# First batch in quarters of columns, one-pass k sketches and shared logits in a sketched-attention and expert-attention kernel

## The chip, the cores and the metric

The kernel runs on one core of a Trainium2 chip. The metric is the device time of one execution in microseconds (us). Engines are named as in the profile: PE is TensorE's matmul, PEld its weight load, DVE is VectorE, ACT is ScalarE, POOL is GpSimd, SP is SyncE, which here issues nearly all DMAs.

## What is computed

The first half is attention by polynomial sketches (4 batches, 4 heads, 1088 positions, width 32, sketch size r = 8, all float32):

```python
def phi(x):
    a = np.einsum('rd,bhsd->bhsr', S1, x)
    b = np.einsum('rd,bhsd->bhsr', S2, x)
    return np.einsum('bhsi,bhsj->bhsij', a, b).reshape(*x.shape[:-1], r * r)
q_p, k_p = (phi(q), phi(k))
kv = np.einsum('bhsf,bhsd->bhfd', k_p, v)
z = np.sum(k_p, axis=2)
num = np.einsum('bhsf,bhfd->bhsd', q_p, kv)
den = np.einsum('bhsf,bhf->bhs', q_p, z)[..., None] + 1e-06
```

Its result, heads side by side, is x (4, 1088, 128). The second half is causal softmax attention with 4 experts, of which each position uses the 2 with the largest logits:

```python
logits = x @ w_gate
topk = np.argpartition(-logits, K, axis=-1)[..., :K]      # K = 2
...
for e in range(E):                                          # E = 4
    scores = scale * ((x @ wq[e]) @ (x @ wk[e]).transpose(0, 2, 1))   # causal mask, softmax -> a
    ye = a @ (x @ wv[e]) @ wo[e]
    out += share_of_expert_e_at_each_position * ye
```

## The kernel before, in words

**Order.** The kernel defines about 1275 small jobs (`job(...)`, each with its engine or a choice of two, what it reads, what it makes and which buffers it holds) and then runs them in the order of a list written out at the top, `ORDER` (lines 21 to 69). A number is a job; "a" or "b" behind it picks the engine. Each engine runs its own jobs strictly in that order, and so does SP with its DMA issues. Buffers come from small pools: 4 PSUM pairs (`ps`), 6 of `w`, 3 of `fp`, and so on. So the list decides both the queues and which buffer is free when.

**Four batches**, each prepared (`prepare`) and then attended (`batch`: `queries`, `scores`, `values`, `outputs`), the preparation of one lying between the attention of the one before.

**Preparation.**
- `sketch` (L501 to L516): q and k, transposed in 32 x 32 blocks by DVE, are multiplied by the sketch matrices in 32 x 32 tiles of the array (L515). The sketch matrix is held as a high and a low part, so each sketch is two passes. Batch 0 does this in two cuts of columns: 34 columns of 32 are split as 4 x 8 columns plus a remainder of 2, so there are 32-wide and 256-wide matmuls; later batches have 288-wide ones.
- `turn_sketch` (L519, DVE) turns the sketches back, `features` (L524, POOL or DVE) makes the 64 products, `sums` (L555, PE) makes kv and z.
- Batch 0 (`attend_rows`): `turn_features` (L589), `numer` (L612: 18 full-array matmuls of 128 rows, the sums of two heads in a block-diagonal tile `kvz`), `divide` (L619 to L621), `turn_x` (L627), `keep_x` (L630 to L635), stores to DRAM (`xd`).
- Later batches (`attend_turned`): the k sums are repeated to all row groups by 4 matmuls with a 0/1 matrix `rep4` (`repeat_sums`, L690) and copied (`keep_repeated`); a fifth sketch column (`fifth`, L696) gives the denominator; `weigh`, `invert`, `scale_first` divide the sketch, then features, `turn_f` (L733), `numer` (L755).
- `choose_experts`: `logits` (L805: 4 matmuls per part of columns, each part computed for both halves of the partitions), `turn_logits` (L809), then comparisons, masks (`store_masks` L890, `fetch_masks` L895: through DRAM, spread to all partitions) and shares (`shares`, `scale_shares`).

**Attention**, three groups of 6, 6 and 5 tiles of 64 positions: `queries` (L958, `pick` L971), `scores` (L996), `take` (L1008, DVE), `soften` (L1024, ACT), `weigh` (L1039, POOL), `turn` (L1044, DVE), `values` (L1072), `outputs` (L1143, L1169, L1193).

**Start of the program.** DVE decodes the sketch matrices; PE runs dummy matmuls (L247: 6 of the 40 dummy jobs are placed, 5 of them before the first sketch); SP and ACT issue the loads of q and k in two parts, SP those of v.

Of the kernel before, what the change touches and what calls it, by code (L numbers as in the profile page):

```python
# [21 lines left out]
0 3 46 4 1 2 48 76 77 82 51 75 42a 22a 49 87 50 45 26b 88 59 86 21a 74 5a 60 16a 61 78 79 54 96 85 81 62a 97 98 89 99a  # L22
80 102a 100b 101a 91 395 107 394 392 83a 84b 111 109 58 391 108a 53 90 24b 66 95a 94b 403 113 112a 110a 92a 393 56 52
104 93b 63 404 103 115 65 106a 105a 117 114b 55 47 398 396 116a 399 402 64 400 401 67b 405 684 121 118 125 407 68 70 406
122 411a 119 126 397 410a 69 57 687 10b 409b 25b 123 127 408a 413 412 124b 13b 120b 414b 130 128a 150 146 31b 151 148
147 416 131 686 154 420a 180 415 149 152 419a 153 155 179 417 162 184a 132 167 168 170 156 418a 163 158 159b 157a 133
181 183a 182 129 169 185 186 421 187 164 165 423 692 215 166a 194 188 422 189 246 195 689 190a 196 216 217 138 191 174
430 424 171 192 431 197a 245 208 432 425 426 428a 209 427a 249a 201 172 685 173 218a 193 202 198 222 247 219 248 223 160
318 250a 251 136 252 429 161a 220 433a 319 224 323a 37b 225a 221 276 434a 175 275 226 322a 277 71 141 140 134 435 176
253 73 8a 203 199 72 321 9b 204a 278 320 254 279b 436 694 227 210 255 324 695 325 438a 256b 177 143 228 205 292 211a  # L30
437a 291 698 456 178a 212 257 293 206 200 258 207 268 700 699 690 137 458 294 213 703a 214 267 457 269 139 701a 260 261
135 280 459 259 284 688 283 229 230 231 460 281 295b 702b 704a 36b 691 270 271b 233a 693 461 262 467 285 272 273 237 706
263b 705 296 462 234a 235a 282 463 297 142 696 232a 286 351 350 697 707b 236 709 708 710 298 711a 713a 327 264 343 352
287b 326 239 265 40b 353 274 342 982 238 712a 714 354a 288 266 328 986 289 473 344 345 468 715 355 290 717 329 472 356
144 475 474 477a 716 19b 723 439 299 464 330b 476a 985 979 443 300 301 346a 302 347 980 331 469 478 303 304 724 357 307a
479 348 334 332 442 335 333 358 977 470 471a 440 306a 718 359 308a 305b 310 309 336 719 311 361 360 725 337 362 508 978
338a 363 441 145 509 364a 312 541 540 510 339 501 983 349 487 315 502 503 504a 365 340 341 313 480 314 366 488 44b 367
316a 481 539 465 511b 538 721a 489 368 726a 543a 720b 722 17b 369 988 512 370 371 513 372 542b 505 373 445 506 490b 374
727a 514 981 544 375 376 545 568 491 377a 569 380a 728 378a 379a 507 482 447 381 444 383 570 553 492 317 571 554 576 382
494 495 483b 577 496 34b 484 987 493 497a 498 578 729 485 555 731a 486 515 384 516 730b 579 584 585 499 586 517 500 518a  # L40
991 519 749 993 750 612 520 751 521 32b 546 587 556a 611 547 992 580a 615a 241 754 385 572a 752 581 557 989 996a 446 558
559 613 614 466 548 573 549b 386 242 240 448 616a 574 760 617 588b 450 589 550 753 453 984 582 997a 583 761 33b 522 451
551 618 29b 523 524 243b 525a 561 528a 628 575 590 995b 452 560 454 526a 529 762 530 627 652 532 755 527a 629 562 651
654 591 653 994a 563 552 564a 531 619 388 655 630 656 620 643 621 631b 635 565 644 622 766 566 763 244 636 645 567 637
657a 632 646 658 756 767 455 623b 765 768 633 592 593 647b 449 659 594 595 770b 624 596 597 757 764a 638 732 769b 648
736 771 772 634 649 639a 601a 533 625 660 598a 650 599a 787 640 602 734 535 641 788 780 794 534 789 603 600b 735 795 604
626 808 536a 733 781 801 642 389 782 773 998 802 605 809 810 999 661 11b 783a 662 663 387 737 1000b 664 665 774 775 803
666 811a 990 1002 43b 804b 667 758 668 796 669 790b 812 784 6b 671a 813 785 739 797a 805 1001 1003 1005a 1006b 831 673a
1004a 832 672b 670a 791 834 814 836a 798 675 833 792 744 799 674 835a 12b 806 786 1007 738 837 838 1009 677 1008 676 905
1016 846 847 800 793 839 776b 28b 853 854 840 741 848 777 807 855 904 841 1010 849a 907 909a 537 778 878 850 851 740 856  # L50
1017 908a 877 1018 779 1011 842b 879 759 861 843 880 862 1012 743 1019b 881a 863 857a 844 906 678 910 1014a 815 864 858
816 845 911 865a 817 27b 1013a 1020a 390 818a 819a 679 869 1015 921 870 1021 882 883 859 35b 823 680 820a 821b 920 7b
822 852 866 681 871 922 1022 606 867 1024a 1023a 936 868 937 884 945 872 860 1042 944 938 1043 912 1044 15b 824 873b 30b
1047 747 929 913 1045 746 874 928 608 742 825 607 923 1046 914 748 930 947 1132 875 1048 939 946 1129 915 948 1131 609a
876 916b 1130 940a 1025 1053 1049 1134b 917 949 950a 885 1051 931 1133b 745 886 918 1027 951 887 941 1026 942 888 932a
610 952 924a 1028 919 889 890 933 39b 1135 934 828 953 827 925 1029 1054 892b 1136 896 826 943 891a 1176 894a 829a 1175
893b 14b 897 926 935 1137 1177 1151 1152 1055 1159 895 1144 1178 1153 1160 898 1204 1138 927 1145 1202 1161 1203 1179b
1139 1207b 1206a 1205 1162 1154 1180 954 955 956 1146 1155b 1056 957 958 1052 1057b 1208 1156 1181 18b 959 960 1147a 961
1163a 1182 1035 1164 1148 1140b 962 1209 1227 1165 963a 1167 1141 1166 967 1030 830 1142 965b 683 966a 1226 1168 1149
964a 968 1228 1169 1157 1143 1235 1033 1234 970 1236 1031 1219 1037 1218 969 1229 1220 1058 1170 1237 1171a 1150 1050  # L60
1230b 899 1242 1158 1243 1172 1231 1244 1040 1059 38b 23b 1039 682 1061 1221 901 1210 1232 1211 900 1222a 1233 1062b
1063b 1064 1238b 1212 902a 1060 1245 1065 1173 1174 971 1032 1223 1213 1246 1224 1073 1214a 972 1080 1215 1247 1041 1081
1074 1239 1225 1216 1240 1082 1248a 1087 1249 1217 1094 1095 1083a 1036 1034 1250 1241 1088 1183 1075 1251 1184 1084
1089 1185 1101 1066 1186 1067 1068 1102 973 1187 976 1252 1076b 1188 1038 1069a 1253 1103 974 1189a 1104b 1070 1193 1105
1085 1096 1077 1190b 41b 903 1254 1071 1255 1194 1090a 1097a 1256 1191b 1106 1091 1196 1192a 1257 1098 1195 1258 1259
1260 1198 1099 1264a 1107 1078 1072 1261b 1100 1086 1197 1265 1092 1262a 1263a 1079 1199 1267 1093 1108 1109 1110 1266
# [48 lines left out]
def kernel(  # L115
# [80 lines left out]
    def a_us(n):  # L196
        return 0.2 + 0.00073 * n
# [209 lines left out]

    pieces_of = {}  # L410

    def prepare(b, rank):
        early = b == 0
# [869 lines left out]
```

## Time and profile before

| what | us |
|---|---|
| median of 3 runs | 270.88 (270.36 to 271.32) |
| the profiled execution | 270.75 |
| its span, first to last instruction | 269.0 |
| PE busy, its weight loads busy | 259.9, 196.3 |
| DVE, POOL, ACT busy | 215.3, 154.2, 101.8 |

The span is what the profile shows; the execution's own time is 1.75 us more. Busy times are of one engine each and overlap. A matmul that waits in PE's pipeline can count as busy, so the weight loads (PEld) are shown beside it. A row of the chain of waits gives the start, the length, the engine, the tile written (pair is a PSUM pair), the line and the count of instructions; each float32 matmul of L515, L555, L612 and most others is two instructions, each with a weight load of its own.

### The profile page before, as it was taken

Reading aid. Unit: us, or ns where it says so; the run is one execution under the profiler, and the core shown is the slowest. Engines: PE = TensorE matmul, PEld = TensorE weight load, DVE = VectorE, ACT = ScalarE, POOL = GpSimd, SP = SyncE. Lnnn points to the kernel's source line nnn. Section 1 sums busy time; section 2 is a strip of 40 time slices with the busy share of each in tenths; the row PEclk is TensorE's granted clock in tenths of the full one; section 3 lists DMA queues with packets and bytes.
Section 4 is the critical chain, followed back from the end, with each engine's and each line's share of the span. In section 5 each row is a group of like instructions: output and inputs, shape, how many; then the busy total and the mean of one; then the engine's idle time right before and its main releaser. Section 6 shows DMA issues by size and latency. Waiting matters only on the chain.

```text
span 269.0 us, 9743 instructions
## 1 busy us (share of the span) xinstructions
PE 259.9 (97%) x4081; PEld 196.3 (73%) x4081; DVE 215.3 (80%) x536; ACT 101.8 (38%) x275; POOL 154.2 (57%) x245
## 2 busy tenths in 40 slices
PE   8599989999999999999999999999999999999994
PEld 3388846557586896586499976764796885789994
DVE  5887799999979986989998249998879389994342
ACT  2131226744433607513814333445604416244030
POOL 5563539776887835369576237864256554262740
PEclk9859999999999999999999999999999999999999
DMA  6958549980587344891550197140380365930002
GB/s 199 191 108 124 114 81 212 172 148 16 100 154 131 92 139 95 157 109 40 135 88 13 34 188 177 19 111 0 67 165 0 75 155 116 173 81 3 5 29 56
DMA packets 80588, 27.38 MB, mean 102 GB/s; under 512 B 49760, under 2 KB 79520, under 8 KB 80544
## 3 DMA queue, kind: packets, MB, share of 16 engines
q1 hardware_dynamic: 79952, 26.03, 50.6%
q8 instruction: 32, 0.52, 0.8%
q10 hardware_dynamic: 592, 0.72, 0.8%
q14 instruction: 12, 0.10, 0.1%
HBM read 22.22 MB, written 4.52 MB: 99 GB/s over the span
## 4 chain that ended last, share of the span: by engine, by line
PE 80%; DVE 14%; issue 3%; POOL 1%; ACT 0%; DVEq 0%; ACTq 0%
PE pair L1072 26%; PE pair L996 21%; PE pair L958 8%; PE pair L1193 6%; PE pair L515 4%; PE pair L555 3%; PE pair L1143 2%; DVE w L1008 2%; DVE qs L971 2%; PE pair L612 2%; PE pair L247 2%; PE pair L589 1%; DVE AT L1044 1%; PE pair L755 1%; DVE w L519 1%
## 5 line engine op out<-in xcount | busy, mean ns | idle before, releaser
L1039 POOL TENSOR_SCALAR w<-w,rs,sh 128x192 f32<-128x192 f32 (+15 forms) x68 | 56.3, 834 | 47.0 <-DVE rs L1035 43.7
L996 PE MATMUL pair<-xT,qs 128*128 128x384 f32 (+10 forms) x216 | 72.9, 476 | 0.7 <-DVE ch L876 0.6
L1024 ACT ACTIVATE w<-w,mx 128x192 f32<-128x192 f32 (+15 forms) x68 | 52.5, 772 | 40.9 <-DVE mx L1008 38.6
L996 PEld LDWEIGHTS pair<-xT,qs 128*128 128x128 f32 x216 | 38.3, 190 | 25.5 <-issue 11.0
L1044 DVE STREAM_TRANSPOSE AT<-w 128x384 f32<-128x384 f32 (+16 forms) x68 | 50.6, 757 | 1.8 <-POOL w L1039 1.7
L1008 DVE CUSTOM_DVE_ANT_0 w<-pair,mask 128x768 f32<-128x768 f32 (+14 forms) x68 | 48.0, 721 | 1.6 <-PE pair L996 1.0
L1072 PEld LDWEIGHTS pair<-AT,xra 32*128 32x128 f32 x1136 | 41.5, 185 | 4.3 <-DVE rs L1035 1.9
L1072 PE MATMUL pair<-AT,xra 32*128 32x160 f32 (+5 forms) x1136 | 44.3, 302 | 0.0
L1099 POOL TENSOR_TENSOR agg<-agg,mb 128x768 f32<-128x768 f32 (+1 forms) x22 | 34.1, 1561 | 16.6 <-ACT agg L191 8.3
L191 ACT COPY agg<-pair 128x384 f32<-128x384 f32 (+1 forms) x36 | 15.1, 466 | 68.5 <-PE pair L1072 54.9
L958 PE MATMUL pair<-xT,Mq 128*128 128x384 f32 (+1 forms) x96 | 33.7, 476 | 0.0
L524 POOL TENSOR_TENSOR fp<-w 128x576 f32<-128x576 f32 x22 | 27.2, 1252 | 9.9 <-DVE w L519 9.5
L971 DVE COPY_PREDICATED qs<-mb,pair 128x768 f32<-128x768 uint16 (+1 forms) x24 | 23.1, 963 | 6.7 <-DMA mb<-md 5.9
L1072 PE MATMUL pair<-AT,xrb 32*128 32x160 f32 (+5 forms) x752 | 26.7, 286 | 0.0
L1072 PEld LDWEIGHTS pair<-AT,xrb 32*128 32x128 f32 x752 | 26.3, 185 | 0.1
L958 PEld LDWEIGHTS pair<-xT,Mq 128*128 128x128 f32 x96 | 17.4, 190 | 10.8 <-issue 2.7
L1193 PEld LDWEIGHTS pair<-Mo,agg 128*128 128x128 f32 x168 | 20.4, 192 | 2.2 <-issue 0.7
L1193 PE MATMUL pair<-Mo,agg 128*128 128x128 f32 x168 | 21.5, 278 | 0.0
L1095 DVE COPY_PREDICATED agg<-mb,pair 128x384 f32<-128x384 uint16 (+1 forms) x24 | 13.1, 557 | 8.7 <-ACT agg L191 8.6
L515 PE MATMUL pair<-in,SK 32*32 32x288 f32 (+2 forms) x544 | 13.4, 377 | 3.1 <-issue 3.1
L1032 POOL TENSOR_SCALAR rs<-zs 128x1 f32<-128x1 f32 x28 | 6.0, 213 | 14.1 <-ACT w L1024 9.3
L519 DVE STREAM_TRANSPOSE w<-pair 128x576 f32<-128x576 f32 x16 | 11.7, 759 | 2.1 <-PE pair L515 2.1
(161 smaller groups left out, 302.2 us busy)
## 6 DMA issues: line engine op xcount, KB each, us to landing
mb<-md SPq DMA_DIRECT2D x7, 576.0 KB, 6.2
xrb<-xd SPq DMA_DIRECT2D x16, 192.0 KB, 6.5
xra<-xd SPq DMA_DIRECT2D x16, 192.0 KB, 6.0
xrc<-xd SPq DMA_DIRECT2D x16, 160.0 KB, 3.8
mb<-md SPq DMA_DIRECT2D x4, 480.0 KB, 6.8
in<-in_q_dram SPq DMA_DIRECT2D x3, 544.0 KB, 5.9
in<-in_k_dram SPq DMA_DIRECT2D x12, 136.0 KB, 3.8
xd<-w SPq DMA_DIRECT2D x12, 136.0 KB, 4.2
```

The lines of the kernel that those rows point to most:

```text
L515: nc.tensor.matmul(dst if early else dst.rearrange("p (j t) -> p j t", t=32), SK[rows, 1] if s else first_[rows], part(src[rows], g), star ...
L524: VEC[e].tensor_tensor(out=f, in0=a[:, :, None, R : 2 * R].to_broadcast([128, NJ, R, R]), in1=a[:, :, 0:R, None].to_broadcast([128, NJ, R, ...
L958: nc.tensor.matmul(plan[ps[x]][:, y, 0:w], Mq[:, ((1, 2), (0, 3))[x][y]], plan[xT][:, 64 * t0 : 64 * t1], start=True, stop=True)
L971: nc.vector.copy_predicated(chosen(), rows(c), rows(plan[ps[x]]))
L996: nc.tensor.matmul(plan[p][:, y, 0 : c1 - c0], plan[qs][:, 128 * t : 128 * t + 128], plan[xT][:, c0:c1], start=True, stop=True)
L1008: nc.vector.tensor_tensor_reduce(out=o, in0=src, in1=msk, scale=-1.0, scalar=mx[:, b, i, x - 1 : x] if x else 3e38, op0=ALU.add, op1=ALU.m ...
L1024: nc.scalar.activation(out=a, in_=a, func=ACTF.Exp, bias=mx[:, b, i, last : last + 1], scale=-1.0, accum_out=zs[:, b, i : i + 1])
L1039: nc.gpsimd.tensor_scalar(out=a, in0=a, scalar1=rs[:, b, i : i + 1], scalar2=plan[("sh", b)][:, i : i + 1], op0=ALU.mult, op1=ALU.mult)
L1044: nc.vector.transpose(dst[:, 0 : keys // 32, t], plan[A][:, 0:keys].rearrange("p (j s) -> p j s", s=32))
L1072: nc.tensor.matmul(plan[Vk[g // 2]][:, g % 2, lo : 32 * nt], plan[(f"xr{j // 12}", b)][rows, j % 12], a[rows, j, lo:], start=(j == 0), sto ...
L1099: nc.gpsimd.tensor_tensor(out=a, in0=a, in1=plan[mb][:, 2 * x : 2 * x + 2, 0:w], op=ALU.mult)
L1193: nc.tensor.matmul(plan[p][0:m, 0, 128 * x : 128 * x + 128], plan[agg][:, e, 128 * x : 128 * x + m], Mo[:, e], start=(e == 0), stop=(e == ...
```

## The change

1. **Batch 0 in quarters.** The 34 columns are split as 9, 8, 9, 8, and the turned q and k keep a gap of zeros, so that the sketch of batch 0 is one cut of 288 columns. The loads of q and k are two equal halves; v comes in 4 loads in place of 4 and a remainder of 2. Numerators: two 64-row matmuls of 33 columns in place of one 128-row matmul of 66.

```diff
+    quarters = (0, 9, 17, 26, C)
-            c0, c1 = (0, 512, S)[x : x + 2]
+            c0, c1 = (0, S // 2, S)[x : x + 2]
...
-            cuts = [(0, 32 * NJ, lambda a, g: a.rearrange("p (j g t) -> p j g t", g=4, t=32)[:, :, g])]
-            if early:
-                cuts = [(32 * N8, 32, lambda a, g: a[:, 128 * N8 + 32 * g : 128 * N8 + 32 * g + 32]),
-                        (0, 32 * N8, lambda a, g: a[:, 32 * N8 * g : 32 * N8 * g + 32 * N8])]
+            both = nm == "k" and not early
+            for s in range(1 if both else 2):
+                for h in range(H):
...
+                        part = src[rows, 32 * NJ * g : 32 * NJ * g + 32 * NJ]
...
             for y in range(2 * x0, 2 * x1):
-                nc.tensor.matmul(plan[t][:, z // 6, c : c + 2 * (D + 1)], f[:, y],
-                                 plan[kvz][:, y % 2].rearrange("p x d -> p (x d)"), start=True, stop=True)
+                c = (D + 1) * (y - 2 * x0)
+                for x in range(2):
+                    rows = slice(64 * x, 64 * x + 64)
+                    nc.tensor.matmul(plan[t][:, x, c : c + D + 1], f[rows, y], plan[kvz][rows, y % 2], start=True, stop=True)
...
-            copy(e, o[:, 0 : 4 * N8].rearrange("p (g j) t -> p j g t", g=4)[:, x0 : x0 + n], src[:, 0:n])
-            if x1 > N8:
-                copy(e, o[:, 4 * N8 :], src[:, n, 0 : C - 4 * N8])
+            for g in range(2):
+                m = x1 - x0 if g == 0 else n
+                copy(e, o[:, :, 9 * g + x0 : 9 * g + x0 + m], src[:, :, g, 0:m])
```

2. **Later k sketches in one pass.** The high and low parts stand side by side in one 32-column matrix `SKk` (made once by a new job, `both`), and the two halves of the result are added after turning back (two jobs a batch, POOL or DVE):

```diff
+        def add_low(e, x):
+            a = parts_ab("k")[:, 2 * x : 2 * x + 2].rearrange("p h j y -> p (h j) y")
+            VEC[e].tensor_tensor(out=a[:, :, 0 : 2 * R], in0=a[:, :, 0 : 2 * R], in1=a[:, :, 2 * R :], op=ALU.add)
```

3. **The repeated sums** of the later batches go through DRAM: one store and 4 loads on SP in place of 4 matmuls and two copies; `rep4` is gone.

```diff
-                nc.tensor.matmul(plan[rep[r // 2]][:, r % 2, 0 : 2 * D], rep4[rows].rearrange("p g f -> p (g f)"),
-                                 plan[kvs][rows, :, 0:D], start=True, stop=True)
+            nc.sync.dma_start(out=plan[kvr][32 * g : 32 * g + 32].rearrange("p r m d -> p r (m d)"),
+                              in_=kd[b].rearrange("(r p) y -> p r y", p=32))
```

4. **Logits made once** (later batches): the lower partitions hold tiles 0 to 8, the upper ones 8 to 16, so 4 matmuls of 288 columns in place of 8, one turn in place of two, comparisons and shares on 9 columns in place of 17; 4 mask stores in place of 2, 4 mask fetches in place of 3, and shares are placed by 4 small operations in place of one.

```diff
+        def logits_by_half(t):
+            for c in range(4):
+                t0 = (NT - HALF) * (c // 2)
+                xv = plan[xT][:, 64 * t0 : 64 * (t0 + HALF)].rearrange("p (t h s) -> p h t s", h=2, s=32)
+                nc.tensor.matmul(plan[t][32 * c : 32 * c + 32, 0, 0 : 32 * HALF].rearrange("p (t s) -> p t s", s=32),
+                                 wg, xv[:, c % 2], start=True, stop=True)
...
+        def place_shares(e):
+            a = plan[ch][:, 0:HALF].rearrange("p t k -> p k t")
+            for x in range(2):
+                for y, t0, t1 in ((0, 0, HALF), (1, HALF, NT)):
```

5. **A new `ORDER`** for all jobs. At the start of the program one dummy job (2 matmuls) is left, behind both sketches of batch 0. SP issues two quarters of v ahead of the last half of k, where the remainder of v stood. On PE, "sketch k1" stands ahead of batch 0's numerators, the turns of the weights behind them, and "sums 1.0" behind batch 0's logits. "keep w" and all copies of x of batch 0 are on ACT. Of the 32 feature jobs 22 were on POOL and 10 on DVE; now 23 are on POOL (two more of q, one less of k) and 9 on DVE.

304 lines of the change are left out of this document (169 added, 135 removed).

## The prediction

> **What bounds the kernel now.** I read the profile page first, then the busy times by stage, then the chain of waits in order of time, and only then single stretches of the timeline.
>
> ```profile
> span 269.0 us, 9743 instructions
> PE 259.9 (97%) x4081; PEld 196.3 (73%) x4081; DVE 215.3 (80%) x536; ACT 101.8 (38%) x275; POOL 154.2 (57%) x245
> PE 80%; DVE 14%; issue 3%; POOL 1%; ACT 0%; DVEq 0%; ACTq 0%
> q8 instruction: 32, 0.52, 0.8%
> ```
>
> The span is 269.0 us and this execution took 270.75 us, so 1.75 us lie outside it; the median of the runs shown, 270.88 us, is 0.13 us more. The chain that ended last is TensorE (PE) for 80%. PE's 97% is not proof by itself, because a matmul that waits can count as busy; so I cut the span into stages.
>
> ```profile
> 0.00:32.00 32.00, 27.57 (x563) 20.83 (x567) 23.28 (x51) 7.09 (x16) 17.82 (x40) 0.89 0.73 149
> 32.00:67.00 35.00, 34.13 (x494) 21.10 (x484) 34.18 (x114) 17.78 (x52) 23.30 (x50) 1.00 0.72 125
> 122.70:265.60 142.90, 142.80 (x2134) 112.54 (x2134) 109.12 (x258) 55.29 (x146) 75.87 (x102) 1.00 0.39 79
> ```
>
> The columns are PE, PE's weight loads, VectorE (DVE), ScalarE (ACT), GpSimd (POOL), granted clock, DMA share, GB/s. Three regimes: up to 32 us nothing is full, and a dependency chain makes the x of batch 0. From 32 to 67 us DVE is busy 34.18 of 35 us and PE's weight loads only 60% of it: DVE sets the pace. After that weight loads fill 79% and DVE 76%: PE's own rate sets the pace, and a matmul less is time gained.
>
> The chain in order of time (start, length, what):
>
> ```profile
> 6.19 3.05 PE pair L515 x127
> 9.23 3.12 issue
> 18.62 2.36 PE pair L555 x72
> 21.56 1.53 PE pair L612 x12
> 24.84 2.82 PE pair L612 x24
> 31.79 0.45 PE pair L805 x8
> 67.21 0.45 PE pair L690 x8
> 105.37 1.48 PE pair L755 x38
> 109.00 1.53 PE pair L515 x63
> 110.53 1.05 PE pair L805 x16
> 155.75 0.17 PE pair L690 x8
> ```
>
> L515 is the sketches, L555 the k sums, L612 batch 0's numerators, L805 the logits, L690 the repeated sums, L755 the later numerators. I take batch 0's logits, at 31.79 us, as the end of the startup.
>
> **The change, step by step: startup.** A sketch matmul costs 24 ns whatever its width: 127 in 3.05 us where half are 32 columns wide, 63 in 1.53 us where all are 288. One cut in place of two drops 64 of the 128 for q and for k: 1.5 us each. The 3.12 us "issue" in the middle of k's sketch waits for no semaphore.
>
> ```profile
> 6.12 3.12 PE L515 MATMUL pair<-in,SK 32*32 32x32 f32 x209
> 9.20:12.30 3.10, 0.03 (x5) 0.00 (x0) 3.10 (x4) 0.00 (x0) 3.00 (x4) 0.96 1.09 243
> 12.30:18.80 6.50, 6.45 (x71) 4.97 (x70) 4.38 (x6) 2.82 (x4) 4.17 (x6) 0.50 0.74 128
> q8 instruction: 1, 0.02, 2.3%
> ```
>
> Up to the stall PE had begun 209 sketch and 4 other matmuls and 10 dummies, each with its load: 446 instructions. The last row is the DMA view of 9.3 to 13 us; the view of 5 to 9.3 us has no such queue at all. The page's 32 packets in 0.52 MB are 16 KB each, about a 32nd of PE's 2 x 4081 instructions, so I read this as PE's next 255 instructions arriving late, behind input loads that fill the DMA engines (share 1.09). The new PE order has 300 instructions up to the end of batch 0's first four groups of transposes (128 sketch matmuls, 4, 2 dummies, 16 transposes), so the same point falls in the k sums, where the inputs have landed. I cost the stall at 0 afterwards. [...] The same rows show PE at half clock (0.50) from 12.3 to 18.8 us, dummy matmuls or not. The new order keeps 2 of 12 dummies, behind the sketches, so sketch q may run at half rate: at most +1.5 us, hidden, since DVE reads q's result only after turning k.
>
> What comes next is DVE and the loads:
>
> ```profile
> 7.80 0.71 DVE L480 STREAM_TRANSPOSE in<-in 128x512 f32<-128x512 f32 x1 [0.39 <-DMA in<-in_k_dram]
> 9.77 2.80 DVE L524 TENSOR_TENSOR fp<-w 128x576 f32<-128x576 f32 x3
> 14.69 1.45 DVE L519 STREAM_TRANSPOSE w<-pair 128x576 f32<-128x576 f32 x2 [2.12 <-PE pair L515]
> 15.62 2.83 POOL L524 TENSOR_TENSOR fp<-w 128x576 f32<-128x576 f32 x2 [2.24 <-DVE w L519]
> 14.51 2.42 PEld L589 LDWEIGHTS pair<-ident,fp 128*128 128x128 f32 x12 [0.81 <-issue]
> ```
>
> - SP now issues two v quarters (131 + 147 KB) ahead of k's last half, where two 16 KB pieces stood: 246 KB more at 243 GB/s is 1.0 us. That half is turned at 8.8 instead of 7.80 us, until 9.5.
> - DVE then runs back q (0.72), features (0.93), back q, features, back k, features, back k, two features, two turns of k1 (0.75 each, as k's 0.71 with up to 64 columns more). Back k starts at 12.8 (before: 14.69); the last k features end at 17.1, the turns at 18.6.
> - POOL makes two q features from 10.2 and 11.9 (1.42 at most), so q is complete at 13.3.
> - PE: 16 feature transposes at half clock, 0.2 us each (12 in 2.42), to 16.5; sums of 36 instructions, 1.18 each, the second from 17.1 to 18.3; the one-pass sketch of k1, half of 1.53, from 18.6 to 19.4.
>
> The numerators follow. Before: 36 full-array instructions, 4.35 us in all (1.53 + 2.82), starting at 21.56 and, with other work between, ending at 27.66. After: 72 instructions of 64 rows, in pairs.
>
> ```profile
> 21.53 1.42 PEld L612 LDWEIGHTS pair<-kvz,fp 128*128 128x128 f32 x12 [0.21 <-ACT kvz L191]
> 27.59 0.52 PEld L390 LDWEIGHTS pair<-AT 64*128 64x128 f32 x8
> 27.67 0.65 PE pair L390 x8
> ```
>
> Full weight loads come every 112 ns ((1.42 - 0.19)/11, one lasting 0.19), 64-row ones every 47 ns ((0.52 - 0.19)/7). So 72 x 47 = 3.4 us, against 4.35. Ends: 72 x 33 = 2.4 us by L555's rate, 72 x 81 = 5.9 us by L390's chain row, which holds a pipeline's start over only 8. I take 3.4, the same shape. Numerators run from 19.4, with the last feature transposes (0.2) between: end 23.0, not 27.66. Turning the weights (6 transposes of the shape of L627's, 9 of which take 1.20) and the last divide (L621 with two small operations, 0.95 as taken) stand before turning x.
>
> ```profile
> 28.24 1.20 PE L627 MATMUL pair<-ident,w 128*128 128x128 f32 x9
> 29.31 1.60 DVE L191 COPY xT<-pair 128x384 f32<-128x384 f32 x2
> 28.17 0.56 DVE L621 TENSOR_TENSOR w<-pair,den 128x384 f32<-128x384 f32 x1
> 23.42 0.96 DVE L191 COPY AT<-pair 128x768 f32<-128x768 f32 x1 [1.81 <-PE pair L379]
> 29.48 0.78 ACT L191 COPY xT<-pair 128x256 f32<-128x256 f32 x2 [0.46 <-PE pair L627]
> ```
>
> Here the change loses something: keep w (0.96 on DVE before) and all three copies of x, two instructions each, go to ACT, one after another: 23.7 + 0.9 + 3 x 0.85 = 27.2 us (0.85 between DVE's 0.80 and ACT's 0.78, which had fewer columns, and a second instruction). Before, two went to DVE. Sums 1.1 lie beside that; sums 1.0 (1.18) now stand behind the logits. With half a microsecond for handovers the logits come at 27.7 to 28.5, 28.1 as taken, against 31.79: **-3.7 us**. Bounds: -5.5 (ACT's copies at the shortest row, numerators at 2.4) and -1.5 (k's load another microsecond later, numerators at 5.9).
>
> **32 to 67 us.** k2's sketch (-0.76), the logits (-0.5) and repeated sums leave PE, which has slack there; DVE decides. It loses one logit transpose of two, a mask copy of 768 columns (0.96 by keep w's row) to ACT, and gets one x copy (0.8 by batch 0's) and the share placement or reciprocals in another place: 0, between -2 and +2, the sizes of two such operations. If the new order used up PE's slack, PE's 40% idle weight-load time is the most there is to win; I allow 4 us.
>
> **67 to 265 us**, where PE counts: sketch k3 -0.76 (half of 1.53), logits 2 and 3 -0.52 each (half of 1.05), repeated sums 2 and 3 -0.45 and -0.17. **-2.4 us.** The copies of the repeated sums on ACT go as well, off the path.
>
> **What is added.** "Add low" (128 x 288, two a batch), four share placements for one, five DMA issues for the repeated sums, two more mask stores and one more fetch.
>
> ```profile
> L524 POOL TENSOR_TENSOR fp<-w 128x576 f32<-128x576 f32 x22 | 27.2, 1252 | 9.9 <-DVE w L519 9.5
> L719 POOL TENSOR_TENSOR w<-w 128x144 f32<-128x144 f32 x6 | 2.9, 490 | 1.8 <-DVE rs L1035 1.1 <-DVE w L519 0.4
> md<-cT SPq DMA_DIRECT2D x8, 8.0 KB, 1.6
> vp<-in_v_dram SPq DMA_DIRECT2D x12, 128.0 KB, 3.8
> DVE qs L971 <- DMA mb<-md: 5.9, 3, 4.2
> ```
>
> - Add low lies between 490 and 1252 ns: 0.75 on POOL, 1.5 a batch; the shares at most 4 x 0.49. POOL is busy 53% of the last stage, so 0 there. If that cover goes, see the third rival.
> - The sums' way through DRAM takes two landings, 3.2 to 7.6 us by the md and vp rows. Numerators 2 stood 38 us behind repeated sums 2 (67.21, 105.37): hidden; the cover is gone only if SP holds a piece back for 30 us. Queued on SP behind the waiting store are batch 0's x fetches and masks; if it waits, the pick of queries waits with them, 1 us per 1 us.
> - The mask stores add two SP issues of under half a microsecond before a fetch that DVE already waits for, 5.9 us in three places: at most 1 us a batch, taken as 0 because the fetch itself is unchanged in bytes.
>
> **Sum.** 270.75 - 3.7 - 2.4 = 264.65, and with the 0.13 to the median, rounded: **264.7 us**.
>
> **Rivals.**
> 1. *The stall stays*, because it was no late instructions. Sketch k would end at 9.5 + 1.5 + 3.1 = 14.1, so back k starts at 14.1 instead of 12.8: +1.3, 266.0. For it: the stall names no cause. Against: the instruction queue's packet right at it. [...] 0.10.
> 2. *The 64-row numerators are not cheaper.* Nothing gained from pairs: 5.9 instead of 3.4 us, 267.2. For it: L390's 81 ns. [...] Against: full-array numerators before went over to 32-row sketches with no gap in the chain, and 64-row weight loads do come at 47 ns. 0.08.
> 3. *POOL becomes the bound* and the kernel gets slower. In each batch's preparation POOL gets 1.5 (add low) and up to 1.8 (shares), and two of the q features move to it from DVE over the program (2.5). If POOL had no room, all of it would delay weigh, then turn A, then the values: 3 x 3.3 + 2.5 less the DVE time freed (2 x 0.93) = 10.5, hence about 275; with room in half the places, 270 to 272. It decides where POOL is full: it has 23.3 of 35 us in the DVE stage, so the point is reached only if a 10 us run of it is above nine tenths and lies on the path. 0.13.
> 4. *The new order also closes PE's gaps* between 32 and 67 us: up to 4 us more, 260.7. For it: PE has fewer instructions to place. Against: DVE is full there. 0.14.
>
> **How the numbers follow.** The forecast has 0.55. The range runs from 260.0 (rival 4, or the startup at -5.5 with DVE at -2) to 270.0 (startup at -1.5 and +2 on DVE, rivals 1 and 2, the mild form of 3); about 0.08 lies above and 0.07 below. A measurement of this kernel tells 0.3%, 0.8 us, from no change: faster than 270.1 has 0.84, within 0.8 us 0.04 and slower 0.12, nearly all of rival 3.
>
> **What would show it.** Right: no "issue" of 3 us in the first 15 us; logits of batch 0 at 28 us; numerators' weight loads about 47 ns apart; the k sketch of batch 3 half of 1.53 us; no PE wait on the later numerators. Wrong: a late landing of k or v (k's turn after 10 us), ACT's x copies over 1 us each, half clock still at the numerators (all their loads twice as long), POOL at nine tenths or more for over 10 us with PE waiting on turn A, or DVE waiting longer for masks.

## The result, and the profile after

The changed kernel takes 272.93 us (median of 20 runs, 271.04 to 276.31), the kernel before 270.72 us beside it (20 runs, 269.08 to 272.29). The ratio is 1.0077, with a 95% interval of 1.0055 to 1.0099: slower by 0.8%. The prediction was 264.7 us, range 260 to 270, with 0.84 for faster: wrong in sign, and the time lies outside the range. Ratios and intervals, here and below, leave disturbed executions out, so they can differ a little from the quotient of the medians. The profiled execution took 271.38 us, near the low end of its kernel; its span is 269.4 us. Its traces can therefore explain 0.6 us of the loss (270.75 for the profiled execution before); for the other 1.6 us there is no trace.

From the page of the changed kernel (busy times of the engines, the chain by engine, the instruction queue):

```profile
PE 254.1 (94%) x3834; PEld 192.1 (71%) x3835; DVE 213.0 (79%) x533; ACT 102.2 (38%) x273; POOL 156.5 (58%) x257
PE 65%; DVE 18%; DMA 7%; issue 3%; POOL 2%; SPq 2%; ACT 0%; DVEq 0%; ACTq 0%; POOLq 0%
```

PE lost 5.8 us of busy time (259.9 before), and the span did not get shorter. PE's share of the chain that ended last fell from 80% to 65%, and DVE, DMA and SP took the rest. The same three stretches as in the prediction, in the changed kernel (PE, PE's loads, DVE, ACT, POOL, granted clock, DMA share, GB/s):

```profile
0.00:32.00 32.00, 23.16 (x397) 18.53 (x402) 21.19 (x46) 10.09 (x24) 16.65 (x39) 0.89 0.79 157
32.00:67.00 35.00, 33.79 (x477) 20.79 (x468) 33.12 (x110) 16.79 (x49) 24.20 (x49) 1.00 0.63 120
122.70:265.60 142.90, 141.68 (x2112) 110.99 (x2111) 109.81 (x260) 52.23 (x137) 77.89 (x113) 1.00 0.39 80
```

At the start PE is busy 4.4 us less (23.16, before 27.57; ten dummy matmuls alone were 4.25 us before), yet the stretch is no shorter. The chain in order of time says where it went (L527 sketches, L535 features, L610 turned features, L576 k sums, L634 numerators, L827 logits of batch 0, L713 fifth column, L768 later numerators, L1014 queries):

```profile
1.63 4.32 DMA in<-in_q_dram
...
5.98 0.76 DVE w L497
...
6.75 0.56 DVE SK L193
...
7.34 0.76 DVE w L497
...
8.14 2.47 PE pair L527 x56
...
11.51 3.40 POOL fp L535 x2
...
16.92 2.38 PE pair L576 x72
...
20.17 1.46 PE pair L634 x24
...
21.99 3.88 PE pair L634 x48
...
31.70 0.51 PE pair L827 x8
...
67.94 0.41 PE pair L713 x8
...
108.63 1.48 PE pair L768 x38
...
130.67 3.08 PE pair L1014 x8
...
136.93 2.22 PE pair L576 x72
```

Two rows of the chain before, to set beside it (L696 is the fifth column, L996 the scores):

```profile
67.66 0.34 PE pair L696 x8
...
122.71 8.49 PE pair L996 x24
```

Batch 0's logits stand at 31.70 us (before 31.79). Nothing of the forecast 3.7 us came, although the 3 us "issue" in k's sketch is gone. The fifth column of batch 2 stands at 67.94 (before 67.66), and the kernel ends no earlier.

### The profile page after: what moved, and what is told of

Read it like the earlier page. It is cut to its first block, busy times and chain, and to the rows that moved or that the text cites. A ratio compares the mean times of both kernels' runs of the same rounds, so it can differ in the third digit from the quotient of the medians.

```text
span 269.4 us, 9287 instructions
## 1 busy us (share of the span) xinstructions
PE 254.1 (94%) x3834; PEld 192.1 (71%) x3835; DVE 213.0 (79%) x533; ACT 102.2 (38%) x273; POOL 156.5 (58%) x257
## 4 chain that ended last, share of the span: by engine, by line
PE 65%; DVE 18%; DMA 7%; issue 3%; POOL 2%; SPq 2%; ACT 0%; DVEq 0%; ACTq 0%; POOLq 0%
PE pair L1128 20%; PE pair L1052 18%; PE pair L1014 6%; PE pair L1249 6%; DVE AT L1100 3%; PE pair L576 3%; DVE qs L1027 3%; DVE w L1064 3%; DMA mb<-md 2%; PE pair L527 2%; PE pair L634 2%; PE pair L1199 2%; DMA in<-in_q_dram 2%; DMA mb<-me 2%; DMA xd<-w 1%
## 5 line engine op out<-in xcount | busy, mean ns | idle before, releaser
L1052 PE MATMUL pair<-xT,qs 128*128 128x384 f32 (+11 forms) x216 | 74.7, 479 | 0.9 <-DVE qs L1027 0.4
L1095 POOL TENSOR_SCALAR w<-w,rs,sh 128x768 f32<-128x768 f32 (+14 forms) x68 | 56.0, 829 | 31.1 <-DVE rs L1091 29.9
L1080 ACT ACTIVATE w<-w,mx 128x768 f32<-128x768 f32 (+16 forms) x68 | 52.5, 772 | 48.7 <-DVE mx L1064 37.0
L1052 PEld LDWEIGHTS pair<-xT,qs 128*128 128x128 f32 x216 | 37.8, 190 | 26.5 <-issue 10.1
L1100 DVE STREAM_TRANSPOSE AT<-w 128x256 f32<-128x256 f32 (+15 forms) x68 | 50.7, 757 | 2.4 <-POOL w L1095 2.4
L1064 DVE CUSTOM_DVE_ANT_0 w<-pair,mask 128x1024 f32<-128x1024 f32 (+14 forms) x68 | 48.0, 723 | 3.6 <-PE pair L1052 3.3
L1128 PEld LDWEIGHTS pair<-AT,xra 32*128 32x128 f32 x1136 | 41.8, 185 | 4.2 <-issue 1.6
L1128 PE MATMUL pair<-AT,xra 32*128 32x160 f32 (+5 forms) x1136 | 44.6, 302 | 0.0
L193 ACT COPY agg<-pair 128x384 f32<-128x384 f32 (+1 forms) x34 | 14.2, 470 | 58.8 <-PE pair L1128 57.3
L1014 PE MATMUL pair<-xT,Mq 128*128 128x384 f32 (+1 forms) x96 | 34.3, 478 | 0.8 <-DVE mx L1064 0.8
L535 POOL TENSOR_TENSOR fp<-w 128x576 f32<-128x576 f32 x23 | 28.6, 1260 | 4.8 <-DVE w L530 3.7
L1128 PE MATMUL pair<-AT,xrb 32*128 32x160 f32 (+5 forms) x752 | 27.1, 286 | 0.0
L1128 PEld LDWEIGHTS pair<-AT,xrb 32*128 32x128 f32 x752 | 26.6, 185 | 0.4 <-issue 0.4
L1014 PEld LDWEIGHTS pair<-xT,Mq 128*128 128x128 f32 x96 | 17.2, 190 | 13.2 <-DVE mx L1064 2.6
L1027 DVE COPY_PREDICATED qs<-mb,pair 128x768 f32<-128x768 uint16 (+1 forms) x24 | 23.0, 960 | 3.5 <-ACT w L1080 1.5
L1088 POOL TENSOR_SCALAR rs<-zs 128x1 f32<-128x1 f32 x32 | 6.8, 212 | 16.8 <-ACT w L1080 14.8
L193 DVE COPY agg<-pair 128x320 f32<-128x320 f32 (+1 forms) x12 | 6.0, 503 | 13.0 <-PE pair L1128 8.4
L1080 ACT ACTIVATION_READ_ACCUMULATOR w<-w,mx 128x1 f32 x68 | 12.8, 188 | 0.0
```

The source lines that it names most:

```text
L193: (nc.scalar.copy if eng == "ACT" else VEC[eng].tensor_copy)(o, i)
L535: VEC[e].tensor_tensor(out=f, in0=a[:, :, None, R : 2 * R].to_broadcast([128, NJ, R, R]), in1=a[:, :, 0:R, None].to_broadcast([128, NJ, R, ...
L1014: nc.tensor.matmul(plan[ps[x]][:, y, 0:w], Mq[:, ((1, 2), (0, 3))[x][y]], plan[xT][:, 64 * t0 : 64 * t1], start=True, stop=True)
L1027: nc.vector.copy_predicated(chosen(), rows(c), rows(plan[ps[x]]))
L1052: nc.tensor.matmul(plan[p][:, y, 0 : c1 - c0], plan[qs][:, 128 * t : 128 * t + 128], plan[xT][:, c0:c1], start=True, stop=True)
L1064: nc.vector.tensor_tensor_reduce(out=o, in0=src, in1=msk, scale=-1.0, scalar=mx[:, b, i, x - 1 : x] if x else 3e38, op0=ALU.add, op1=ALU.m ...
```

## The experiments

Theory A: the parts save time and the new order loses it. Theory B: the parts themselves cost, and the order is neutral. "Old order" puts each new job beside the job that it belongs to; "new order" is that of the change.

| kernel | median us | ratio to before | 95% interval |
|---|---|---|---|
| the change | 272.93 | 1.0077 | 1.0055 to 1.0099 |
| all parts, old order | 289.94 | 1.07 | 1.0653 to 1.0747 |
| no parts, new order | 278.04 | 1.0295 | 1.0252 to 1.0339 |
| the change, old start | 275.45 | 1.0189 | 1.0152 to 1.0226 |
| the change, new start, old order after it | 288.2 | 1.0656 | 1.0615 to 1.0696 |
| quarters alone, old order | 269.64 | 0.997 | 0.9948 to 0.9993 |
| shared logits alone, old order | 269.31 | 0.9962 | 0.994 to 0.9984 |
| sums by DRAM alone, old order | 273.47 | 1.0113 | 1.0081 to 1.0146 |
| one-pass sketch alone, old order | 277.19 | 1.0258 | 1.0216 to 1.03 |
| one-pass sketch, additions left out | 269.66 | 0.9979 | 0.9956 to 1.0002 |
| one-pass sketch, additions on DVE | 274.13 | 1.015 | 1.0109 to 1.0191 |
| quarters and shared logits, old order | 268.45 | 0.9933 | 0.9905 to 0.9961 |
| the change without one-pass | 273.3 | 1.0103 | 1.0062 to 1.0144 |
| the change without DRAM sums | 278.65 | 1.0209 | 1.0152 to 1.0265 |
| the change, additions left out | 272.09 | 1.0049 | 1.0023 to 1.0074 |
| the change with dummies | 272.95 | 1.0112 | 1.0073 to 1.0151 |
| the change with a mended start | 272.87 | 1.0084 | 1.0051 to 1.0116 |
| the change, less on DVE | 273.61 | 1.0105 | 1.0067 to 1.0143 |
| mended start, less on DVE | 274.78 | 1.0155 | 1.0107 to 1.0204 |

### Parts and order apart

```diff
 ORDER: repeat S2 | ... | back k1.1 | back k1.0 | ...     (of before)
+ORDER: ... | back k1.1 | add low 1.1 | back k1.0 | add low 1.0 | ...
-ORDER: ... | repeat sums 1 | keep rep 1.0 | keep rep 1.1
+ORDER: ... | store sums 1 | repeat sums 1.0 | 1.1 | 1.2 | 1.3
```

> All parts of the change (quarters, one-pass k sketches, logits made once, repeated sums through DRAM), but the jobs in the order of before: new jobs stand beside the jobs that they belong to, six dummy jobs as before. Theory A (the parts save time, the new order loses it): no stall in k's sketch, batch 0's logits at 29 to 30 us instead of 31.7 to 31.8, and 2.4 us less on PE afterwards, so 266 to 268.5 us, faster than before (270.7) by 0.8 to 1.7%. Theory B (the parts themselves cost, by DRAM round trips, 64-row numerators or GpSimd's added work; the order does nothing): 272 us or more, as the changed kernel (272.9). The numerators run at full clock here, 20 to 24 us into the span: 47 ns each (3.4 us in all) if the half clock made them dear, 61 to 81 ns if their shape does.

```diff
-code of the change, ORDER of the change
+code of before, ORDER of the change (removed jobs put back beside their neighbours)
```

> None of the parts: the code of before, with its jobs in the new order (the two jobs of repeated sums and their copies put where the fifth column is made; one dummy job). Theory A (the order loses): slower than before by what the order costs, 274 to 277 us, since the 2.4 us that PE saves are missing as well. Theory B (the parts cost): 270 to 271.5 us, like before.

```diff
-ORDER of the change, jobs up to batch 0's last turn of logits
+the same jobs in the order of before, its dummy jobs included
```

> The changed kernel, but the 130 jobs up to batch 0's last turn of logits stand in the order of before (with its dummy matmuls), the rest in the new order. If the new order loses at the start of the program: logits at 29 to 30 us, the whole 269.5 to 271 us, 2 to 3 us below the changed kernel. If it loses between 32 and 79 us: 272 to 273 us, as the changed kernel, whatever the start gains.

```diff
-ORDER of the change, jobs behind batch 0's logits
+the same jobs in the order of before
```

> The counterpart: the changed kernel with its own start (up to batch 0's logits) and the order of before from there on. If the new order loses at the start: 269.5 to 271 us. If it loses after 32 us: logits at 31.7 us, then 2.4 us saved, 267.5 to 269 us.

Both theories fall. All parts in the old order take 289.94 us, and the old parts in the new order 278.04: both mixtures are worse than either matched pair. Order and parts are fitted to each other. The two kernels that change orders at batch 0's logits (275.45 and 288.2 us) lie above every time that was expected of them. The kernel of 289.94 us has a fault of its own, which its chain shows: the sums' store and loads stood in a block on SP, ahead of a mask fetch.

```profile
167.38 2.34 DMA kd<-kvs
169.74 0.32 SPq L704
...
172.69 0.38 SPq L945
173.12 6.09 DMA mb<-me
...
179.40 1.02 DVE qs L1027
```

The loads (L704) wait for the landing of the store, the mask fetch (L945) stands behind them, and pick (L1027) behind that. The kernel with the new start and the old order behind it (288.2 us) has the same block: there the store lands for 2.32 us and the mask fetch behind it for 6.28. So these two runs price a placement as well as the parts, and each part was then tried alone.

### Each part alone, in the old order

```diff
-for s in range(2):                    # k sketch of batches 1 to 3
+for s in range(1):                    # SKk: high and low part side by side
+job(f"add low {b}.{x}", ...)          # on POOL, behind each turn back
```

> The kernel before with one part alone: the later k sketches in one pass, their halves added on GpSimd right behind the turn back. If an order that is not fitted to a part turns its added work into waits: PE saves 3 x 0.76 us, but each add low (0.75 us and a handover) stands between the turn back and the k features on GpSimd's queue; where k features are late on the path the kernel loses 1 to 2 us a batch: 271 to 275 us. If the added work is hidden, as the prediction had it: 269 to 270 us.

```diff
-lparts = [[(0, 9), (9, NT)]]
+lparts = [[(0, HALF)]]                # with the mask stores, fetches and shares of the change
```

> The kernel before with one part alone: logits made once (4 mask stores, 4 mask fetches, shares placed by 4 operations). If the mask path is on the critical path: two more stores and one more fetch a batch make pick wait longer, 1 to 2 us in each of three batches, 273 to 277 us. If they are hidden, as the prediction had it: PE saves 2 x 0.52 and the turn of logits, 269 to 270.5 us.

```diff
-repeat sums b: 4 matmuls, 2 copies
+store sums b behind the fifth column; repeat sums b.0 to b.3 ahead of the first turn of features
```

> The kernel before with one part alone: the repeated sums through DRAM, stored behind the fifth column and fetched ahead of the turn of features. If SP's queue hides it, as the prediction had it: 269.5 to 271 us. If SP holds up behind the store's landing (2.3 us measured for it in the run with all parts), what is queued behind it is late: 1 to 3 us a batch, 273 to 279 us.

```diff
-cuts of 32 and 256 columns, full-array numerators
+quarters of 9, 8, 9, 8 columns, 64-row numerators
```

> The kernel before with one part alone: batch 0 in quarters with 64-row numerators, six dummy jobs as before. If the prediction's startup steps hold in an undisturbed order: k's sketch without the 3 us stall, batch 0's logits 1.5 to 3.7 us earlier than 31.79, the whole 267 to 269.5 us. If the 64-row numerators take 5 us and more and the rest waits for the loads: logits at 31 to 33 us, the whole 270 to 273 us.

Two parts gain (quarters 0.3%, shared logits 0.4%) and two lose: DRAM sums 1.1%, the one-pass sketch 2.6%, dearer than either expectation. With the quarters alone batch 0's logits come at 29.73 us, 2.1 earlier than before, and less than half of that is left at the end. With the DRAM sums alone, the profiled execution (272.31 us) has batch 0's logits 1.2 us earlier than before, yet is 0.8 us late at the fifth column of batch 2 (68.42, before 67.66). So the loss begins between these two points; the wait that brings it is open. The chain of the one-pass sketch alone shows the price of "add low" (L546; L525 turns back, L530 features, L571 k sums, L821 logits):

```profile
24.83 0.78 DVE w L525
...
25.78 0.55 POOL w L546
...
27.26 2.83 POOL fp L530 x2
...
31.52 1.31 PE pair L571 x36
32.84 0.45 PE pair L821 x8
...
108.29 1.48 PE pair L771 x38
...
113.53 0.69 DVE w L525
...
114.30 0.80 POOL w L546
```

It stands between the turn back and the features, features and sums follow on queues that keep their order, and batch 0's logits wait behind the sums: 1.0 us later than 31.79. By batch 2's numerators (batches count from 0) the kernel is 2.9 us late (108.29, before 105.37), and at 114 us the same link is on the path again. GpSimd is not full (158.7 of 274.4 us busy), so on this reading the cost is one more link in a chain, not load.

```diff
-features read the sum of both halves (add low)
+features read the high half alone; the low halves are left out
```

> The kernel before with the one-pass k sketch, but without add low: the low halves of the later k sketches are left out of the features, so that the price of the additions alone is seen against the run with them (277.2 us). If the additions and their handovers cost the 7 us: 268 to 270 us, PE's 2.3 us gained in part. If the one-pass sketch itself disturbs the order (its result comes at another time, other waits): 273 us and more.

```diff
-add low on POOL
+add low on DVE
```

> The kernel before with the one-pass k sketch and add low on VectorE, right behind the turn back, in place of GpSimd. If the 7.5 us of add low are the handover and GpSimd's queue: 270 to 272 us, since VectorE gets 2.4 us more over the program and GpSimd nothing. If they are the work itself on the way to the features: 275 us or more, as on GpSimd (277.2).

Without the additions 269.66, with them on DVE 274.13, on POOL 277.19 us. So PE's saving is worth about 0.2%, which its interval (0.9956 to 1.0002) does not tell from nothing, and the additions cost 4.5 us on DVE and 7.5 on POOL; the sketch itself disturbs nothing. The time on DVE lies between the two that were expected (270 to 272, or 275 and more): an addition costs on either engine, and which engine takes it makes 3 us.

```diff
 ORDER of before
+quarters and shared logits; two-pass sketches and matmul sums as before
```

> The old order with the two parts that gained alone (quarters -0.6, shared logits -1.0): if the gains lie in different stages and add up, 268.4 to 269.0 us, faster than before by 0.5 to 0.7%. If both only fill the same slack ahead of batch 0's masks, 269.2 to 270.

268.45 us, 0.67% below before (0.39 to 0.95%): the two gains add up, and this version beats both kernels. From its page:

```profile
span 265.4 us, 9528 instructions
PE 256.6 (97%) x3964; PEld 193.6 (73%) x3965; DVE 214.1 (81%) x538; ACT 101.7 (38%) x275; POOL 153.9 (58%) x253
PE 81%; DVE 9%; DMA 5%; SPq 2%; issue 1%; ACT 0%; ACTq 0%
```

PE has 2.5 us more to do than in the change, and the span is 4.0 us shorter: PE holds 81% of the chain.

### Parts undone in the new order

```diff
-both, add low 1.0 to 3.1; one-pass k sketches
+two-pass k sketches
```

> The changed kernel with one part undone: the later k sketches in two passes, without the two add low a batch and without the job that makes the joined matrix; the rest of the new order kept. If the add low wait on the path costs in the new order too: 269 to 271.5 us, below the changed kernel's 272.9 by 1 to 4 us. If the new order hides it and PE is the bound: 3 x 0.76 us more, 274 to 276 us.

```diff
-store sums, repeat sums b.0 to b.3
+repeat sums b, keep rep b.1, keep rep b.0 (ScalarE), ahead of fifth b
```

> The changed kernel with one part undone: the repeated sums by 4 matmuls and two copies on ScalarE, put where the fifth column is made, in place of one store and four loads on SP. If SP's queue and the landings cost in the new order too: 269.5 to 272 us. If they are hidden there: 3 x 0.4 us more PE time, 273.5 to 275 us.

```diff
-add low 1.0 to 3.1 in the new order
+features read the high half alone; the low halves are left out
```

> The changed kernel without add low: the low halves of the later k sketches are left out of the features, so that its price in the new order is seen. If add low is on the path there too: 269 to 271 us, 2 to 4 us below the changed kernel, and 2.5 us or more below the run with two-pass sketches in the new order (273.3). If the new order hides it: 272.5 to 273.5 us, and something else takes the gain.

Without the one-pass sketch 273.3 us: its interval (1.0062 to 1.0144) overlaps that of the change (1.0055 to 1.0099), so no gain or loss of the part can be told there. Additions left out: 272.09, with intervals that overlap; the new order hides them for the most part. The matmul sums, put where I put them, are slower than DRAM (ratio 1.0209), although DRAM lost in the old order. None of these three brings the new order below before (quarters and shared logits were not undone in it), and the price of a part belongs to the order that it stands in.

### The start of the new order

```diff
 ORDER of the change: room | load S1 | idle | ...
+five dummy jobs on PE ahead of decode
```

> The changed kernel with five dummy jobs (10 matmuls) put back ahead of everything else on PE, as before had them; nothing else moved. If the half clock falls on the numerators because PE has done nothing in the first 8 us: the half-rate time comes before 19 us, the numerators take 4.3 us instead of 5.3, batch 0's logits come at 29.5 to 30 instead of 31.7, and the whole is 271 to 272 us. If the half clock has nothing to do with the dummies, or later stages give the gain back: 272.5 to 273.5 us, as the changed kernel.

```diff
+five dummy jobs on PE ahead of decode
-DVE:  decode | turn q0.1 | spread3 | turn q0.0
+DVE:  decode | spread3 | turn q0.1 | turn q0.0
-POOL: pick8 | clear q | const | ident | clear k | mask | spread1 | onehot | rep16
+POOL: clear q | clear k | const | spread1 | ident | rep16 | pick8 | q's features | mask | onehot
```

> As the run with dummies put back, and the copies that q's sketch needs ahead of other work again: VectorE's spread before the turns of q, GpSimd's clear, constants and spread first, mask and one-hot after q's features. If the late sketch of q (8.14 instead of 6.12 us) costs as much as it is late: logits at 28 to 28.5 us and 269.5 to 271 us. If the loads or GpSimd's features end the wait instead: no difference to the run with dummies alone.

The numerators first, in three kernels. The change (granted clock 0.50):

```profile
24.00:30.00 6.00, 6.00 (x40) 5.38 (x41) 2.74 (x6) 2.30 (x5) 2.63 (x5) 0.50 0.98 163
```

Quarters alone in the old order (chain, and granted clock 1.00):

```profile
19.40 1.50 PE pair L634 x24
...
22.80 2.80 PE pair L634 x48
```

```profile
22.00:26.00 4.00, 4.00 (x88) 3.46 (x85) 3.71 (x11) 0.00 (x0) 1.90 (x2) 1.00 0.74 116
```

At full clock the 72 instructions take 1.50 + 2.80 = 4.30 us, 60 ns each: as long as the 36 full-array ones before (4.35). With the half clock on most of them they take 1.46 + 3.88 = 5.34. The dummies did not move the half clock away: with them the numerators still take 1.46 + 3.90 us, at a granted clock of 0.50 from 23 to 29 us (and from 8 to 13 us the granted clock is 0.66 as well), and the whole is 272.95. In the profiled execution with the mended start they ran at full clock: no weight load of theirs took over 188 ns, in the change up to 336 (L827 is batch 0's logits):

```profile
7.85 2.47 PE pair L527 x56
...
19.87 1.46 PE pair L634 x24
...
21.70 2.80 PE pair L634 x48
...
29.81 0.51 PE pair L827 x8
...
66.93 0.41 PE pair L713 x8
...
107.63 1.48 PE pair L768 x38
...
137.49 2.22 PE pair L576 x72
```

So the logits of the new start can come at 29.8 us (29.49 in the run without the one-pass sketch, with a granted clock of 1.00 from 20 to 30 us); the sketch of q was brought forward by only 0.3 us, because q's landing ended the wait (at 6.40 us, 5.95 in the change). Still the kernel took 272.87 us. Against the change the execution is 1.9 us ahead at the logits, 1.0 at 67 and at 108 us, and 0.6 us behind at 137 us. One caution: the next kernel with this same start had the half clock on its numerators again (3.86 us for 48) and its logits at 32.10, so the start's gain comes in some executions only. Over all profiles, one execution each, the granted clock from 19 to 31 us is 0.72 or 0.73 in nine of the 13 kernels with quarters, 0.86 in one and 1.00 in three; in the seven kernels without quarters it is 1.00.

What lies between 108 and 137 us (before, then the change, then the change with the mended start; columns as above):

```profile
107.00:138.00 31.00, 30.93 (x338) 21.15 (x341) 29.12 (x75) 14.39 (x36) 20.53 (x32) 1.00 0.56 100
```

```profile
107.00:138.00 31.00, 30.24 (x316) 18.66 (x314) 30.27 (x76) 14.74 (x39) 21.85 (x29) 1.00 0.52 114
```

```profile
107.00:138.00 31.00, 28.93 (x292) 17.33 (x292) 30.29 (x74) 14.46 (x37) 21.51 (x29) 1.00 0.48 108
```

In the new order DVE is busy 98% of this stretch and PE's loads 60% or less (before 94% and 68%). The chain is off PE from 115.56 to 130.67 us in the change, 15.1 us; before, from 113.11 to 122.71, 9.6 us. That suggested that DVE takes back the gain, so nine copies were moved from DVE to ScalarE, without and with the mended start:

```diff
-keep x 2.1, base 2.0.0, keep V 1.0.0, 1.1.0, 1.2.0, 1.2.2, base 2.1.0, keep x 3.1, keep V 2.0.2 on DVE
+the same nine on ACT
```

> The changed kernel with nine copies of batches 1 to 3, 0.5 to 1.1 us each, on ScalarE in place of VectorE (x, base and sums copies between 110 and 190 us); nothing else moved. VectorE is busy 98% from 113 to 131 us and from 165 to 185 us there, ScalarE 36 to 44%. If VectorE's full stretches take back what the start and PE's saved matmuls gain: 1.5 to 3 us less, 270 to 271.5 us. If the stretches are full but not what sets the end: 272.5 to 273.5 us, as the changed kernel.

> The same nine copies on ScalarE in the kernel with the mended start (batch 0's logits at 29.8 instead of 31.7 us, yet 272.9 us as a whole). If VectorE's stretches gave the start's gain back: 269 to 270.5 us, below the run without the mended start by 0.5 to 1.5 us. If not: no difference between the two.

273.61 and 274.78 us: no gain, rather a loss, so that theory falls in this form. What DVE waited for between 108 and 194 us, in the change and then with less on DVE (total us, times, longest):

```profile
DVE agg L1151 <- ACT agg L193: 0.3, 1, 0.3
```

```profile
DVE agg L1151 <- ACT agg L193: 11.5, 3, 7.7
```

The copies now stand in ScalarE's queue, and DVE stands still behind them for 11.5 us. Taking work off the full engine only moved the wait. What would free this stretch stays open; an order planned anew was not tried.

A second stretch off PE, from 142.0 to 185.2 us in the change, is a rival that the traces can answer. Its chain goes through DRAM: batch 2's x is stored, and SP's fetches of x wait for that store with a mask fetch behind them (the change, then the mended start, where L1128 is the values and L1052 the scores):

```profile
152.03 3.93 DMA xd<-w
...
156.99 4.07 DMA mb<-me
...
185.21 5.53 PE pair L1052 x14
```

```profile
143.19 15.86 PE pair L1128 x428
```

With the mended start PE holds these 15.86 us of the chain, the way through DRAM is off it, and the kernel is no faster (272.87 us). By these two executions the detour runs level with PE's own work and does not explain the loss.

## Why the prediction was wrong, step by step

- **The sum.** In the profiled execution the logits come 3.6 us later than the forecast 28.1: 0.8 are there when the numerators begin (20.17, forecast 19.4), 2.1 more when they end (25.88, forecast 23.0), and 0.7 arise in the turns and copies behind them. Of the 2.4 us behind 67 us nothing came either. These two terms, 3.7 and 2.4 us, are the steps that failed.
- **The stall in k's sketch: right that it goes, its cause open.** No 3 us "issue" is left, in the change or with quarters alone, and k's last half is turned at 9.30 to 10.04 us (forecast 8.8 to 9.5). Rival 1 is out. In before and in five experiments with its start the stop comes after the same 209 sketch matmuls, whether it lasts 1.27 us (one-pass sketch alone) or 3.56 (the same with the additions left out). In the old parts with the new order all 256 run through in 6.40 us without it, so the quarters are not needed to lose it; there the DMA share from 9.3 to 12.3 us is 0.34 (before 1.06). That fits instructions that arrive late behind input loads, and does not prove it.
- **24 ns a sketch matmul whatever its width: misread.** The chain's row counts 127 of the matmuls of that time; 209 began in 3.12 us, 15 ns each. With 288 columns 64 take 1.60 us (quarters alone), 25 ns each. By these rows the sketches of q and k took about 4.2 us of PE at full clock before (3.12 and half of 2.23, which ran at a granted clock of 0.50) and take 3.2 now: about 0.5 us saved a sketch, not 1.5.
- **q was left out of the sum.** I took the start of q's sketch as unchanged. It went from 6.12 to 8.14 us: on DVE the first turn of q, which waited for q's landing (until 5.95 us), now stands ahead of a copy of the sketch matrix, and that (6.75) ahead of the other turn. POOL's two features took 3.40 us, not 2.8, and end at 14.9, not 13.3. PE's queue keeps its order, so the k sums stood behind the transposes of q: 16.92 to 19.30 instead of to 18.3. I had followed the moved jobs on k's way only.
- **Numerators at 47 ns: wrong, as rival 2 had it.** 60 ns at full clock, so 4.30 us, not 3.4. The 47 ns were read from 8 weight loads; the truth lies between that row and the one that I set aside (81 ns), inside the bounds, but the gain is nil. Here twice the instructions (72 for 36) at half the time each (60 ns for 121) come out even.
- **Half clock: in the list of what would show it wrong, not in the sum.** It fell on the numerators and the transposes behind them (granted clock 0.50 from 24 to 30 us): 1.0 us on the numerators alone (5.34 against 4.30). With the late q (0.8) and the numerators' own rate (0.9) it makes up most of the startup's missing 3.6 us; even at full clock, with the mended start, the logits come at 29.81, not 28.1.
- **ACT's copies of x: right.** About 0.8 us a pair of instructions.
- **32 to 67 us at 0: nearly right**, +0.4 (36.24 us from batch 0's logits to batch 2's fifth column, before 35.87).
- **-2.4 us on PE behind 67 us: the other step that failed.** PE's instructions did go (2968 weight loads behind the fifth column, before 3024), but from there to the end the change takes 201.5 us and before 201.3. "A matmul less is time gained" needs PE to set the pace, and in the new order the chain is off PE 5.5 us longer between 113 and 131 us alone, with DVE busy 98%. That this stretch takes back the 2.4 us is the likeliest reading, not shown. In the old order PE's savings do come through (quarters and logits: PE at 81% of the chain).
- **Add low at 0: wrong.** 4.5 to 7.5 us alone in the old order. I hid it under GpSimd's mean load; it is a link in a chain of in-order queues. In the new order it is largely hidden, and so is the gain.
- **DRAM sums at 0: wrong in the old order** (+1.1%), better than matmuls as I placed them in the new one. Its place on SP decides. In the old order the loss begins between 30.6 and 68.4 us.
- **Mask stores at 0: right.** With shared logits alone the kernel gains 0.4%.
- **Rival 3 had the sign and nearly the time (270 to 275), not the mechanism: luck.** POOL is busy 58% and holds 2% of the chain; it did not become the bound.
- **The order.** I treated it as neutral apart from the steps that I followed. The two mixtures show that it is worth as much as the dearest part: 7.5 us for the old parts (278.04 against 270.56 beside it).

Shown: what the parts cost alone, the numerators' rate, the late q, the price of the additions. Argued only: that the 108 to 137 us stretch takes back the start's gain and PE's saving, from pairs of single executions. Open: what sets that stretch, what brings the half clock, and why the median lies 1.6 us above the profiled execution.

## What to carry to other kernels

Where every engine runs a written order, a part has no price of its own: price each part in the order that it will stand in, and try the parts one by one, since here two gained 0.7% together and the other two lost 1.1% and 2.6% alone. Cover for an added operation is not an engine's mean load but the slack of the chain that it is put into; a link of 0.8 us between two engines, twice a batch, cost up to 7.5 us. A rate for 72 instructions is not read from a row of 8.

## What the runs showed of the hardware

- **Half clock on a busy PE.** In the change PE was busy 9.3 of the 10 us from 13 to 23 us (its weight loads 7.75) at full clock, and from 24 to 30 us it got half:

```profile
13.00:23.00 10.00, 9.30 (x178) 7.75 (x172) 9.28 (x14) 3.37 (x10) 5.32 (x6) 1.00 0.55 124
```

  So here it came behind 10 us in which PE counts as busy for 93% of the time; in before it came at 12.3 us, behind a stop of 3.1 us in which PE was busy 0.03. No run shows what brings it. Of the change's 20 executions four had a mean clock of 0.994, and three of these took 271.0 to 271.6 us; those at 0.987 mostly took 272.5 to 274.0.
- **A long product on DVE beside one on GpSimd.** The product of two operands (features, 128 x 576) takes DVE 0.72 us at the shortest in the change and 2.26 us here, beside a product on GpSimd that began just before it:

```profile
127.15 1.65 POOL L1155 TENSOR_TENSOR agg<-agg,mb 128x768 f32<-128x768 f32 x1
127.16 2.26 DVE L535 TENSOR_TENSOR fp<-w 128x576 f32<-128x576 f32 x1
```

  1.65 and a bare 0.72 make 2.37, near the 2.26: as if one went behind the other. That GpSimd held DVE up is my reading of this pair, and no run shows by what. It is not always so: in before, a product on DVE took 0.79 us at 92.18 while GpSimd was at two of its own (91.18 to 94.01). This pair lies in the stretch from 107 to 138 us, in which DVE is busy 98%.
